# LayerNorm statistics moved from VectorE to ScalarE in a fused transformer block, and two sends put ahead of two transposing reads

## The chip, the cores and the metric

The kernel runs on one core of a Trainium2 chip. The metric is the device time of one execution in microseconds (us), the median of several runs. PE is TensorE's matmul side and PEld its weight loads, DVE is VectorE, ACT is ScalarE, POOL is GpSimd, SP the engine whose queue issues the transfers. The granted clock is the share of TensorE's full clock that the profile records, 1.00 being full.

A time is always a little longer than the span that the profile shows (first to last instruction): here by 1.74 to 1.86 us, in one experiment by 2.03 us.

## The reference, cut to what matters

```python
def _layernorm(x, axis=-1, eps=1e-5):
    m = jnp.mean(x, axis=axis, keepdims=True)
    v = jnp.var(x, axis=axis, keepdims=True)
    return (x - m) / jnp.sqrt(v + eps)
...
    # S = 2048 rows, D = 576, 32 heads, 8 dilated window positions, F = 4608
    h = x + attention(_layernorm(x), A_wqkv, A_wo)
    h2 = h + mlp(_layernorm(h), B_w1, B_b1, B_w2, B_b2)   # mlp normalises once more
```

The MLP is GELU (tanh form) between two matmuls. LN2 is the LayerNorm of `h` together with the second one inside the MLP: both fold into one factor, `rstd = (var * (1 + eps) + eps * eps) ** -0.5`.

## The kernel before

The 2048 rows are 16 tiles of 128, handled in eight pairs ("groups"). For each group, PE does MLP-1 (`pm`, 17.7 us), the attention output matmul Wo of the *next* pair (`pw`, 2.2 us) and MLP-2 (`po`, 17.8 us; 15.5 us in the last two groups). While PE does MLP-2 of one group, LN2 of the next pair runs on the other engines, and its result goes to HBM and comes back transposed (`hnT`), because MLP-1 needs it so. DVE is meanwhile busy with the attention of later tiles, whose Exp runs on ACT, in the same queue as the GELU evictions (`hT`).

```python
    def ln2(j):                                   # DVE
        pw = pw_of.pop(j)
        h = sb.tile([P, D], F32, tag="h", name="h", bufs=2)
        nc.vector.tensor_tensor(out=h..., in0=pw[:, :, 0:HALF], in1=x_all[:, j, :]..., op=ALU.add)
        h_of[j] = h
        hn[j] = (h,) + ln_stats([h[:]], "ln2", 1.0 + EPS, EPS * EPS, 2)   # 2 bn_stats, bn_aggr, veps

    # ln2_rstd: GpSimd pow;  ln2_bias: DVE, -mean * rstd;  ln2_hn: ACT, Identity(h * rstd + bias)

    def dma_transpose(dst, src):
        td = dram.tile([P, KT * P], BF16, tag="td", name="td", bufs=4)
        nc.sync.dma_start(out=td[:, 0:D], in_=src)
        nc.sync.dma_start(out=td[:, D:KT * P], in_=src[:, KF * P:D])
        nc.sync.dma_start_transpose(out=dst, in_=td[:])
...
        def ln2_pair(c, d, e, b2=True):
            for j in (c, d):
                ln2(j)
                ln2_rstd(j)
                if j == d:
                    ln2_bias(c)
                    send_h(c)                     # ln2_hn, then dma_transpose
                if b2:
                    add_b2(j)
            if e is not None:
                att_den(e)
            ln2_bias(d)
            send_h(d)
...
    def exps(j):
        att_exp(j)                                # ACT Exp of the logits of tile j
        gelu_table()                              # brings the GELU table back (1.28 us in the trace)
...
        # group 0:  ia[12] = exps(e), Wo of d, ln2_pair(c, d, e, False), ...   during MLP-2
        #           ib[4] = att_qk(f);  ib[32] = exps(f)
        # in the trace ACT keeps the order of the program: the GELU evictions of the next group (from 115.51 us)
        # come behind exps(f) (113.58)
```

The first pair (tiles `A[0]`, `A[1]`) is normalised in the QKV phase by the same helpers and is not touched by the change. So seven pairs change; "the first changed pair" is the one of the second group.

## Time and profile before

| | before |
|---|---|
| time, median of 3 runs | 372.36 us (372.13 to 372.79) |
| span of the profiled run | 370.9 us |
| PE busy | 363.7 us, 98% of the span, granted clock full in every slice |
| DVE, ACT, POOL busy | 316.0, 209.7, 26.5 us |

Part 1 of the page of the kernel before: each engine's busy time, its share of the span, and its number of instructions.

```profile
PE 363.7 (98%) x4944; PEld 300.7 (81%) x4944; DVE 316.0 (85%) x522; ACT 209.7 (57%) x435; POOL 26.5 (7%) x34
```

PE has about 7 us in which it does nothing, 5 of them ahead of the first matmul (1.5) and behind the last (3.6). Taking 20 us from DVE can then give little more than the share of the remaining 2 us that DVE causes. Where that is, the chain that ended last shows (start, duration, what, how often; "issue" is time in which the engine waited for nothing that the profile shows), again of the kernel before:

```profile
113.58 0.42 ACT logits L340
114.01 1.28 ACT L438
115.31 0.20 ACT warm L438
115.51 2.92 ACT hT L465 x8
118.43 0.04 issue
118.47 8.99 PE pm L204 x160
127.46 2.21 PE pw L204 x36
129.67 17.75 PE po L480 x144
147.41 17.79 PE pm L204 x324
```

From 118.47 us to the end the chain is matmuls. In front of that it runs through ACT: an Exp (L340), a GELU table load, eight evictions of the second group. That Exp had waited for DVE, as ACT's timeline of the kernel before shows (start, duration, engine, line, operation, output and input; in brackets the idle time ahead and what ended it):

```profile
95.12 0.42 ACT L340 ACTIVATE logits<-logits 128x256 f32<-128x256 f32 x1 [2.60 <-DVE logits L329]
99.09 0.87 ACT L168 ACTIVATE hn<-h,ln_nmr,ln_rstd 128x576 bf16<-128x576 f32 x1 [2.04 <-DVE ln_nmr L164]
100.52 0.87 ACT L168 ACTIVATE hn<-h,ln_nmr,ln_rstd 128x576 bf16<-128x576 f32 x1 [0.56 <-DVE ln_nmr L164]
...
113.58 0.42 ACT L340 ACTIVATE logits<-logits 128x256 f32<-128x256 f32 x1 [10.89 <-DVE logits L329]
```

In one number: from the first MLP-1 matmul of the second group (109.14 us) to the first Wo matmul behind it (127.28 us) PE took 18.14 us. I call this stretch the *stage*. The later groups, where nothing waits, take 17.7 us.

The SP queue of the kernel before, in the pair of the fourth group (a send is the two DMA_DIRECT2D into `td`, a transposing read the DMA_TRANSPOSE):

```profile
172.62 0.34 SPq L184 DMA_DIRECT2D td<-hn  x1
173.01 0.42 SPq L185 DMA_DIRECT2D td<-hn  x1
174.71 1.21 SPq L186 DMA_TRANSPOSE hnT<-td  x1
176.01 0.53 SPq L184 DMA_DIRECT2D td<-hn  x1
176.59 0.42 SPq L185 DMA_DIRECT2D td<-hn  x1
178.19 1.20 SPq L186 DMA_TRANSPOSE hnT<-td  x1
```

The second tile was ready at 174.7 us, but its send stood in the queue behind the first tile's read, which itself had to wait for the first send to land (the read was issued at 174.71 us, 2.1 us after the send, whose larger part takes 2.0 us to landing). A read lands 2.8 us after its issue (2.7 to 2.9 for those of `hnT`), so the second arrived at about 181.0 us; PE needed it at 185.1.

### The profile page before, as it was taken

The page shows a single profiled execution, that of the slowest core. Times are in us where ns is not written, and L with a number is a line of the kernel's source. Part 1 is how long each engine was busy: PE and PEld are TensorE (multiplying, and loading weights), DVE is VectorE, ACT ScalarE, POOL GpSimd, SP SyncE. Part 2 cuts the span into 40 slices and gives each one's busy share as a digit, 9 for nine tenths or more (in the row PEclk, how much of TensorE's full clock was granted, in tenths as well). Part 3 has the DMA queues.
Part 4 walks back from the last instruction along what each step waited for, and adds up shares of the span by engine and source line. Part 5 has one row for each costly group of instructions (what it writes and reads, how often), then busy time and mean ns, then how long its engine had stood idle before and what let it go on. Part 6 is the DMA issues. An engine that isn't in the chain of part 4 may idle for free.

```text
span 370.9 us, 11469 instructions
## 1 busy us (share of the span) xinstructions
PE 363.7 (98%) x4944; PEld 300.7 (81%) x4944; DVE 316.0 (85%) x522; ACT 209.7 (57%) x435; POOL 26.5 (7%) x34
## 2 busy tenths in 40 slices
PE   7999999999999999999999999999999999999996
PEld 4789877888789977887788778878887788778874
DVE  6799999999999999999999899999999997642332
ACT  2688755798407870867076807681668156505630
POOL 2322004000100020002000200020002000200000
PEclk9999999999999999999999999999999999999999
DMA  7987779955434314620412042203320321030000
GB/s 234 319 241 216 194 208 238 335 184 73 160 89 147 53 34 130 224 47 21 119 53 53 20 102 71 53 19 87 83 56 19 76 62 39 2 87 18 4 0 32
DMA packets 57266, 38.96 MB, mean 105 GB/s; under 512 B 31345, under 2 KB 55537, under 8 KB 57217
## 3 DMA queue, kind: packets, MB, share of 16 engines
q1 hardware_dynamic: 57056, 38.18, 37.7%
q8 instruction: 38, 0.62, 0.7%
q10 hardware_dynamic: 160, 0.07, 0.1%
q14 instruction: 12, 0.09, 0.1%
HBM read 19.92 MB, written 12.42 MB: 87 GB/s over the span
## 4 chain that ended last, share of the span: by engine, by line
PE 71%; DVE 22%; issue 2%; ACT 1%; DMA 1%; POOL 1%; POOLq 0%; DVEq 0%
PE pm L204 31%; PE po L480 24%; PE po L551 8%; PE pw L204 4%; DVE prod L357 3%; DVE prod L318 3%; DVE prod L312 3%; DVE prod L361 3%; DVE ln_stats L144 2%; PE pq L204 2%; DMA kv_ring<-kv_dram 1%; PE busy L636 1%; POOL ln_rstd L155 1%; DVE mx L328 1%; ACT hT L465 1%
## 5 line engine op out<-in xcount | busy, mean ns | idle before, releaser
L204 PE MATMUL pm<-hnT,w_sb 64*128 64x256 bf16 x2304 | 143.2, 269 | 0.6 <-ACT hT L465 0.5
L465 ACT ACTIVATE hT<-pm,b_sb 128x256 bf16<-128x256 f32 (+1 forms) x288 | 108.0, 502 | 34.3 <-PE pm L204 34.3
L204 PEld LDWEIGHTS <-w_sb 64*128 64x128 bf16 x2304 | 113.6, 94 | 14.4 <-issue 2.6
L480 PEld LDWEIGHTS <-hT 128*128 128x128 bf16 x864 | 84.0, 98 | 22.6 <-issue 1.7
L480 PE MATMUL po<-w2a_sb,hT 128*128 128x288 bf16 x672 | 84.5, 286 | 0.0
L204 PE MATMUL pq<-wq_sb,xnT 64*128 64x288 bf16 x768 | 54.0, 283 | 0.4 <-ACT xnT L250 0.2
L204 PEld LDWEIGHTS <-xnT 64*128 64x128 bf16 x864 | 44.0, 94 | 9.2 <-issue 0.4
L155 POOL TENSOR_TENSOR ln_rstd<-ln_veps,mhalf 128x1 f32<-128x1 f32 (+2 forms) x27 | 25.7, 953 | 296.7 <-DVE ln_veps L149 244.6
L318 DVE TENSOR_TENSOR prod<-prod 128x2304 bf16<-128x2304 bf16 (+1 forms) x64 | 44.3, 691 | 2.1
L340 ACT ACTIVATE logits<-logits 128x256 f32<-128x256 f32 x16 | 6.7, 417 | 68.0 <-DVE logits L329 67.9
L357 DVE TENSOR_TENSOR prod<-kv_ring,a 128x4608 bf16<-128x4608 bf16 x16 | 40.9, 2558 | 0.3
L312 DVE TENSOR_TENSOR prod<-kv_ring,q_all 128x4608 bf16<-128x4608 bf16 x16 | 40.8, 2552 | 0.4 <-DMA kv_ring<-kv_dram 0.2
L204 PE MATMUL pm<-hnT,w1h_sb 64*128 64x256 bf16 x288 | 39.5, 269 | 0.0
L361 DVE TENSOR_TENSOR prod<-prod 128x2304 bf16<-128x2304 bf16 (+1 forms) x32 | 33.9, 1058 | 1.1
L480 PE MATMUL po<-w2b_sb,hT 128*128 128x288 bf16 x192 | 25.5, 286 | 0.0
L289 ACT CAST kv_ring<-pq 128x576 bf16<-128x576 f32 x32 | 19.4, 640 | 8.3 <-PE pq L204 8.2
L168 ACT ACTIVATE hn<-h,ln_nmr,ln_rstd 128x576 bf16<-128x576 f32 x16 | 13.9, 867 | 13.5 <-DVE ln_nmr L164 13.5
L204 PE MATMUL pw<-wo_sb,oT 64*128 64x288 bf16 x256 | 19.5, 283 | 0.2
L438 ACT ACT_TABLE_LOAD x14 | 18.0, 1283 | 0.3
L204 PEld LDWEIGHTS <-oT 64*128 64x128 bf16 x288 | 14.1, 94 | 4.0 <-POOLq L214 0.8
L527 DVE TENSOR_TENSOR prod<-hT 128x512 f16<-128x512 f16 (+1 forms) x8 | 3.6, 455 | 16.0 <-ACT hT L465 16.0
L402 DVE TENSOR_TENSOR h<-pw,x_all 128x576 f32<-128x576 f32 x16 | 12.0, 753 | 5.7 <-PE pw L204 5.6
(89 smaller groups left out, 316.1 us busy)
## 6 DMA issues: line engine op xcount, KB each, us to landing
w_sb<-in_B_w_dram SPq DMA_DIRECT2D x6, 768.0 KB, 5.3
kv_ring<-kv_dram SPq DMA_DIRECT2D x28, 144.0 KB, 2.5
w2a_sb<-in_B_w_dram SPq DMA_DIRECT2D x4, 1008.0 KB, 6.6
kv_dram<-kv_ring SPq DMA_DIRECT2D x13, 288.0 KB, 3.9
out_dram<-o_sb SPq DMA_DIRECT2D x15, 144.0 KB, 2.0
td<-q_all SPq DMA_DIRECT2D x14, 144.0 KB, 2.2
td<-hn SPq DMA_DIRECT2D x14, 144.0 KB, 2.0
wq_sb<-in_A_wqkv_dram SPq DMA_DIRECT2D x3, 576.0 KB, 6.7
```

Source lines behind the costliest of these rows:

```text
L155: nc.gpsimd.tensor_tensor(out=rstd[:], in0=veps[:], in1=mhalf[:].to_broadcast([P, n]), op=ALU.pow)
L168: nc.scalar.activation(out=dst, in_=src, func=ACT.Identity, scale=rstd, bias=nmr)
L204: last = nc.tensor.matmul(duo["g"][r ^ swap][i], lhsT=lhsT, rhs=rhs, start=(swap == 0 and i == 0 and kt == 0), stop=(swap == 1 and kt == K ...
L289: pace[0] = nc.scalar.copy(out=dst.rearrange("p (d g h) -> p g d h", g=2, h=H // 2), in_=ps[:, :, 0:HALF].rearrange("p g (h d) -> p g d h" ...
L312: nc.vector.tensor_tensor(out=prod[:], in0=k_ring[j % 2], in1=q_all[:, j, :].unsqueeze(1) .to_broadcast([P, W, D]), op=ALU.mult)
L318: nc.vector.tensor_tensor(out=prod[:, :, o * H:o * H + n], in0=prod[:, :, a * H:a * H + n], in1=prod[:, :, c * H:c * H + n], op=ALU.add)
L357: nc.vector.tensor_tensor(out=prod[:].rearrange("p w (d h) -> p w d h", h=H), in0=v_ring[j % 2].rearrange("p w (d h) -> p w d h", h=H), in ...
L361: nc.vector.tensor_tensor(out=prod[:, 0:n, :], in0=prod[:, 0:n, :], in1=prod[:, n:2 * n, :], op=ALU.add)
L438: nc.scalar.activation(out=warm[:], in_=mhalf[:], func=ACT.Gelu_apprx_tanh)
L465: pace[0] = nc.scalar.activation(out=hT[us[i // GF]][:, GF * r + i % GF, 0:N], in_=ps[:, r, i * N:(i + 1) * N], func=ACT.Gelu_apprx_tanh, ...
L480: nc.tensor.matmul(banks[half], lhsT=hT[f // (2 * GF)][:, f % (2 * GF), i * P:(i + 1) * P], rhs=w2_rows(f)[:, half * HALF:(half + 1) * HAL ...
L551: nc.tensor.matmul(bank, lhsT=l, rhs=r, start=(start and m == 0), stop=(m == NM - 1), skip_group_check=True)
```

## The change

The intent: take LN2's statistics off DVE, which is 85% busy, and give them to ACT, which is 57% busy, as two passes whose sums the engine accumulates; and let the second tile's send go out ahead of the first tile's read.

```diff
-    def dma_transpose(dst, src):
+    def dma_out(src):
         td = dram.tile([P, KT * P], BF16, tag="td", name="td", bufs=4)
         nc.sync.dma_start(out=td[:, 0:D], in_=src)
         nc.sync.dma_start(out=td[:, D:KT * P], in_=src[:, KF * P:D])
+        return td
...
+    def ln2_act(j):
+        h = h_of[j]
+        y = sb.tile([P, D], BF16, tag="hn", name="hn", bufs=2)
+        nmean, var, rstd = (... [P, 1] tiles ...)
+        nc.scalar.activation(out=y[:], in_=h[:], func=ACT.Identity, scale=-1.0 / D, accum_out=nmean[:])
+        nc.scalar.activation(out=y[:], in_=h[:], func=ACT.Square, bias=nmean[:], accum_out=var[:])
+        nc.scalar.activation(out=var[:], in_=var[:], func=ACT.Identity, scale=(1.0 + EPS) / D, bias=eps2[:])
+        nc.gpsimd.tensor_tensor(out=rstd[:], in0=var[:], in1=mhalf[:], op=ALU.pow)
+        hn[j] = (h, rstd, nmean, y)
+
+    def ln2_send(j):
+        h, rstd, nmean, y = hn[j]
+        nc.scalar.activation(out=nmean[:], in_=nmean[:], func=ACT.Identity, scale=rstd[:])
+        ln_apply_act(y[:], h[:], rstd[:], nmean[:])
+        hn[j] = dma_out(y[:])
+
+    def ln2_in(j):
+        nc.sync.dma_start_transpose(out=hnT_slot(j), in_=hn.pop(j)[:])
...
         def ln2_pair(c, d, e, b2=True):
             for j in (c, d):
-                ln2(j)
-                ln2_rstd(j)
-                if j == d:
-                    ln2_bias(c)
-                    send_h(c)
+                ln2_h(j)                          # only the residual addition
+                ln2_act(j)
+            for j in (c, d):
                 if b2:
                     add_b2(j)
+                ln2_send(j)
+            for j in (c, d):
+                ln2_in(j)
             if e is not None:
                 att_den(e)
-            ln2_bias(d)
-            send_h(d)
```

More of the change, by code (lines that the diff above doesn't have):

```diff
@@ L78 @@
     b2_bc = wpool.tile([P, D], BF16, name="b2_bc")
+    eps2 = wpool.tile([P, 1], F32, name="eps2")
     mhalf = wpool.tile([P, 1], F32, name="mhalf")
@@ L185, in dma_transpose @@
         nc.sync.dma_start(out=td[:, D:KT * P], in_=src[:, KF * P:D])
+        return td
+    def dma_transpose(dst, src):
+        td = dma_out(src)
         nc.sync.dma_start_transpose(out=dst, in_=td[:])
@@ L397, in wo_duo, with ln2_h @@
         return make
-    def ln2(j):
+    def ln2_h(j):
         pw = pw_of.pop(j)
@@ L404, in ln2 @@
         h_of[j] = h
+        return h
+    def ln2(j):
+        h = ln2_h(j)
         hn[j] = (h,) + ln_stats([h[:]], "ln2", 1.0 + EPS, EPS * EPS, 2)
+    def ln2_act(j):
+        h = h_of[j]
+        y = sb.tile([P, D], BF16, tag="hn", name="hn", bufs=2)
+        nmean, var, rstd = (sb.tile([P, 1], F32, tag=f"ln2_{t}", name=f"ln2_{t}", bufs=2) for t in ("nmean", "var", "rstd"))
+        nc.scalar.activation(out=y[:], in_=h[:], func=ACT.Identity, scale=-1.0 / D, accum_out=nmean[:])
[10 more added lines that the diff above has]
+        nc.sync.dma_start_transpose(out=hnT_slot(j), in_=hn.pop(j)[:])
     def add_b2(j):
@@ L432, in tr_h @@
         nc.scalar.copy(out=hnT_slot(j), in_=pt)
-    def dma_tr_h(j):
-        dma_transpose(hnT_slot(j), hn.pop(j)[:])
     def gelu_table():
@@ L637 @@
         nc.gpsimd.memset(mhalf[:], -0.5)
+        nc.gpsimd.memset(eps2[:], EPS * EPS)
         make_identity(nc, ident[:])
@@ L696, in pv_t @@
             dma_tr_o(j)
-        def send_h(j):
-            ln2_hn(j)
-            dma_tr_h(j)
         def ln2_pair(c, d, e, b2=True):
             for j in (c, d):
-                ln2(j)
-                ln2_rstd(j)
-                if j == d:
-                    ln2_bias(c)
-                    send_h(c)
+                ln2_h(j)
+                ln2_act(j)
+            for j in (c, d):
                 if b2:
                     add_b2(j)
+                ln2_send(j)
+            for j in (c, d):
+                ln2_in(j)
             if e is not None:
                 att_den(e)
-            ln2_bias(d)
-            send_h(d)
         loads = {v: [c_(load_w1, c)] for c, v in enumerate((3, 4, 9, 14, 16, 18))}
```

## The prediction

> **What bounds the kernel.** TensorE. The page gives PE busy 363.7 of 370.9 us (98%), clock full in every slice. The table of PE's waits holds only 3.0 us, half of it before the first matmul. The last-ending chain looks mixed (PE 71%, DVE 22%), but from 118.47 us to 367.3 us it is matmuls alone, and the DVE part before it runs beside an almost full PE: the only stall that it hands to PE in the MLP is at 118.47 us. There the GELU evictions of the second group start late (115.42 us), because ScalarE's queue holds an Exp that waits 10.9 us for DVE's logits. The MLP-1 pass of that group takes 18.3 us (109.14 to 127.46), the later ones 17.8: about 0.5 us lost.
>
> **What changes** (14 of 16 tiles; the first pair keeps the old way).
> - DVE loses two BATCH_NORM_STATS2 (452 ns each), the aggregate (209), veps (156) and nmr (153): 1.42 us a tile, 20 us in all. DVE busy 316 to about 296 us.
> - ScalarE gains two 576-column passes and two one-column operations. [...] ACT busy 210 to 235-245 us, of 371. No table load is added in the built order.
> - GpSimd keeps one pow a tile (0.55 to 1.0 us).
> - The transfers are the same in number. In a steady pair of before, the sends begin at 172.62 and 176.01 and the transposing reads at 174.71 and 178.19; the second send waits behind the first read though its data was ready at 174.71. Now the second send no longer does.
>
> **On the critical path?** A reading lands 2.8 us after issue, so the second tile arrived at about 181.0, and PE needs it at 185.1. With ScalarE's serial chain (starting after the Exp and the GELU table load end at 171.2) the second normalised tile is ready near 176.9 instead of 174.7; the regrouped sends give back about 1 us; it lands near 182: still 3 us early. In the first changed pair (needed at 109.14) I get 108.1 against 108.45 before; in the last (needed at 333.86) about 332.4 against 332.5. So PE shouldn't wait anywhere. What remains is that DVE runs about 2.5 us earlier after the first changed pair, so the blocking Exp and the GELU evictions start about 2 us earlier and the 0.5 us stall goes.
>
> **Time.** 372.36 - 0.5 = 371.9 us, range 371.3 to 372.7. Faster by over 2%: 0.01, within 2%: 0.98, slower: 0.01.
>
> **What would show it.** DVE near 296 us busy and more idle; ACT near 240; PE busy unchanged near 363.7; the first MLP-1 pass after 109 us at 17.8 us with no wait on hT; no PE wait on hnT's reads; the two hnT reads of a pair issued back to back, the second near 179 in the steady pair. The chain of waits stays PE throughout the MLP.
>
> **What would make it wrong.** If the accumulating passes cost some 0.3 us more each than estimated, the four in series use up the 1.1 and 1.4 us of slack in the first and last changed pair, and PE waits there for hnT by some tenths of a us. If ScalarE were held up further (by pow on GpSimd, or by semaphores between its dependent steps), the same waits would appear in all seven pairs, each adding directly. If earlier DVE work moves halo or weight transfers into collisions, the reads could land late.

Cut from it are the costs of single operations from which ACT's gain was put together, as no trace of the case showed them. They came to 2.0 us a tile, 28 us in all, reading the accumulator left open. ACT's 235 to 245 us, the 176.9 us of the second normalised tile and the landing times (near 182, 108.1 and 332.4 us) rest on this sum, an estimate of mine not taken from the traces; the time, 372.36 - 0.5 = 371.9 us, does not contain it. As to its last sentence, reads do land at different times after their issue: in the changed kernel that of `oT` at 89.41 us took 2.90 us, with 69 GB/s moved meanwhile, that at 145.59 us 4.45 us, with 163 GB/s.

## The result, and the profile after

The changed kernel took 371.69 us (371.56 to 372.19, 4 runs) against 372.25 us (372.07 to 372.79, 4 runs) of the kernel before. A ratio is the mean time of one kernel's runs over that of the other's of the same rounds, so not quite the ratio of the medians that are quoted; here it is 0.9985, interval 0.9968 to 1.0002. Two further batches gave 371.55 us against 372.16 (0.9980, 0.9968 to 0.9993) and 371.68 against 372.37 (0.9987, 0.9974 to 0.9999). So the change is worth a little over half a microsecond: "same" at 2%, as predicted.

Part 1 of the page of the changed kernel:

```profile
PE 363.2 (98%) x4944; PEld 299.4 (81%) x4944; DVE 299.3 (81%) x452; ACT 239.1 (65%) x519; POOL 25.2 (7%) x35
```

DVE lost 16.7 us and ACT gained 29.4 us; PE does what it did. The chain that ended last, in the changed kernel, over the same stretch:

```profile
93.92 14.81 PE po L505 x120
108.72 17.79 PE pm L209 x324
126.52 2.21 PE pw L209 x36
128.72 17.75 PE po L505 x144
```

There is no ACT piece any more: MLP-1 of the second group is one run of 17.79 us, as in all later groups. The stage takes 17.69 us (108.66 to 126.35), 0.45 less than before. ACT's timeline of the changed kernel shows both sides of the trade:

```profile
96.43 0.67 ACT L420 ACTIVATE hn<-h 128x576 bf16<-128x576 f32 x1
97.00 0.19 ACT L420 ACTIVATION_READ_ACCUMULATOR hn<-h 128x1 f32 x1
97.22 0.78 ACT L421 ACTIVATE hn<-h,ln_nmean 128x576 bf16<-128x576 f32 x1
97.90 0.19 ACT L421 ACTIVATION_READ_ACCUMULATOR hn<-h,ln_nmean 128x1 f32 x1
98.12 0.29 ACT L422 ACTIVATE ln_var<-ln_var,eps 128x1 f32<-128x1 f32 x1
...
101.99 0.87 ACT L169 ACTIVATE hn<-h,ln_nmean,ln_rstd 128x576 bf16<-128x576 f32 x1
...
110.40 0.42 ACT L345 ACTIVATE logits<-logits 128x256 f32<-128x256 f32 x1 [6.25 <-DVE logits L334]
```

The second normalised tile is ready at 102.86 us instead of 101.39, later although PE runs 0.5 us earlier in this profile. The blocking Exp starts at 110.40 instead of 113.58. The SP queue of the changed kernel, in the pair of the fourth group:

```profile
175.19 0.34 SPq L185 DMA_DIRECT2D td<-hn  x1
175.58 0.42 SPq L186 DMA_DIRECT2D td<-hn  x1
176.28 0.33 SPq L185 DMA_DIRECT2D td<-hn  x1
176.66 0.42 SPq L186 DMA_DIRECT2D td<-hn  x1
177.22 2.52 SPq L433 DMA_TRANSPOSE hnT<-td  x2
```

The reads are back to back. The second starts at 178.5 us (177.22 + 2.52 less its own 1.2) and, at 2.9 us to landing, arrives near 181.4; PE needs it at 184.1.

The two profiled spans differ by 1.1 us (370.9 and 369.8), which is more than the effect. Half a us of it lies ahead of the change: PE's first MLP-1 matmul came at 69.87 us before and at 69.36 us after, in a part of the program where both kernels do the same but for one small GpSimd memset. In the other two profiles of the changed kernel it came at 69.98 and 70.01 us, in those of the experiments between 69.3 and 70.5. A single pair of profiles therefore cannot be subtracted here; the stage can.

Cut at the same matmuls, the two profiles differ nowhere else on PE's path: from the first MLP-1 matmul to the stage it is 39.27 us before and 39.30 after, from the third group's first MLP-1 matmul to the end of the last matmul 219.91 us in both. Behind the last matmul 3.60 us of the span are left before and 3.46 after. That piece is 3.60 and 3.62 us in e6 and e10, which build on the kernel before, and 3.42 to 3.46 in all the runs that build on the changed kernel, e3 included. So some 0.15 us of what the spans gain is in the closing instructions and not in the stage; no run shows why.

### The profile page after: what moved, and what is told of

Same layout as the page of the kernel before. It is cut to its first block, busy times and chain, and to the rows that moved or that the text cites. A ratio compares the mean times of both kernels' runs of the same rounds, so it can differ in the third digit from the quotient of the medians.

```text
span 369.8 us, 11478 instructions
## 1 busy us (share of the span) xinstructions
PE 363.2 (98%) x4944; PEld 299.4 (81%) x4944; DVE 299.3 (81%) x452; ACT 239.1 (65%) x519; POOL 25.2 (7%) x35
## 4 chain that ended last, share of the span: by engine, by line
PE 84%; DVE 11%; ACT 2%; POOL 1%; issue 1%; POOLq 0%; DVEq 0%
PE pm L209 37%; PE po L505 29%; PE po L576 8%; PE pw L209 5%; PE pq L209 4%; DVE ln_stats L145 2%; DVE prod L323 2%; DVE prod L362 1%; DVE prod L317 1%; PE busy L661 1%; DVE prod L366 1%; POOL ln_rstd L156 1%; ACT hT L490 1%; DVE ln_mv L146 1%; ACT L463 0%
## 5 line engine op out<-in xcount | busy, mean ns | idle before, releaser
L423 POOL TENSOR_TENSOR ln_rstd<-ln_var,mhalf 128x1 f32<-128x1 f32 x14 | 11.3, 810 | 249.8 <-ACT ln_var L422 249.6
L345 ACT ACT_TABLE_LOAD x13 | 16.7, 1283 | 0.2
```

The lines of the kernel that those rows point to most:

```text
L345: nc.scalar.activation(out=logits[:], in_=logits[:], func=ACT.Exp, scale=SCALE)
```

## The experiments

Theory: the whole gain is the stage. DVE finishes the logits of tile f earlier, so the Exp that blocks ACT's queue is earlier, so the GELU evictions of the second group are in time. Rivals: the gain comes from less DVE work, or from earlier reads, in all seven pairs. A second question is why the longer ACT chain costs nothing, and how near it is to costing something.

| run | median, us | before, us | stage, us | PE waits on hnT, us |
|---|---|---|---|---|
| before, profiled | 372.36 | | 18.14 | none |
| changed, e1 and e11 | 371.55, 371.68 | 372.16, 372.37 | 17.69, 17.69 | none |
| e2, first changed pair only | 372.05 | 372.16 | 17.70 | none |
| e3, all but that pair | 372.20 | 372.16 | 18.13 | none |
| e4, Exp ahead of GELUs | 373.79 | 372.16 | 17.68 | 1.47 |
| e5, statistics only | 374.66 | 372.10 | 17.68 | 1.35, 0.66, 1.14 |
| e6, sends only | 372.20 | 372.10 | 18.13 | none |
| e7, one more pass | 373.19 | 372.10 | 17.68 | 0.98, 0.36 |
| e8, two more passes | 386.73 | 372.10 | 20.47 | 3.81, then 1.2 to 1.9 in each pair, 0.29 in the last |
| e9, e4 mended | 372.06 | 372.37 | 17.68 | 1.27 |
| e10, half statistics | 371.98 | 372.37 | 17.69 | none |
| e12, e9 with one table switch | 371.97 | 372.36 | 17.68 | 0.82 |

### e1 and e11: the changed kernel again

No edit; yardsticks of their batches.

> The changed kernel once more, as the yardstick of this batch. Expected 371.7 us, about 0.5 us under the kernel before. The MLP-1 pass of the second group (the run of 324 MLP-1 matmuls that follows the first changed pair) should take 17.8 us, against 18.3 in the kernel before.

> The changed kernel as the yardstick of this batch: 371.6 us, 0.5 us under the kernel before.

Both came as expected, 371.55 and 371.68 us, with the stage at 17.69 us.

### e2 and e3: where the gain sits

```diff
# e2: the first changed pair new, the others as before (ln2_pair_old: statistics, sends and order of the kernel before)
-                ia[0] = ... c_(ln2_pair, c, d, e)]
+                ia[0] = ... c_(ln2_pair_old, c, d, e)]
# e3: the other way round
-                ia[12] = [..., c_(ln2_pair, c, d, e, False), ...]
+                ia[12] = [..., c_(ln2_pair_old, c, d, e, False), ...]
```

> New LN2 for the first changed pair alone, the other six pairs as before. Theory (the whole gain is the removed wait of PE for the GELU evictions of the second group): as fast as the changed kernel, 371.7 us, with a 17.8 us MLP-1 pass in the second group. Rival (the gain comes from less VectorE work, or earlier transposing reads, in all seven pairs): one seventh of it, so 372.2 us.

> The complement: the first pair's LN2 as before, new LN2 for the other six pairs. Theory: no gain, 372.25 us as the kernel before, and the MLP-1 pass of the second group takes 18.3 us again, though DVE's busy time falls by six sevenths of what the whole change took off. Rival: six sevenths of the gain, 371.8 us.

The stage decides it: 17.70 us with that pair alone, 18.13 us with the other six alone, although the six took DVE's busy time from 316.0 to 301.9 us. Six sevenths of the work moved bought nothing on PE's path.

The medians say it less clearly. e3 is level with the kernel before (372.20 against 372.16), as the theory has it. e2 was to be as fast as the changed kernel and came at 372.05, only 0.1 us under before. Its spans explain a part: their mean is 370.12 us, against 370.54 of the kernel before, 370.36 of e3 and 369.84 of e1 in the same batch. But in each of its five runs the time exceeds the span by 2.02 to 2.05 us, where all the others have 1.74 to 1.86. These 0.2 us lie outside the first and last instruction, and no run here says what they are. So e2 by its trace has the gain, by its spans most of it, by its times not clearly; what lies outside the span stays open.

### e6: the sends alone

```diff
# kernel before, statistics on DVE as they were
-            dma_tr_h(j)
+            hn[j] = dma_out(hn[j][:])
...
             send_h(d)
+            for j in (c, d):
+                ln2_in(j)
```

> The kernel before with the regrouped sends alone, statistics on DVE as before. Theory: the second read of each pair is issued 1 to 1.5 us earlier, but nobody waits for it, so 372.25 us as before, and the second group's MLP-1 pass stays at 18.3 us. Rival (earlier reads are the gain): 371.7 us.

372.20 against 372.10 us, stage 18.13: no gain from earlier reads, as nobody waited for them.

### e10: the same DVE time taken away by another way

```diff
# kernel before; wrong result on purpose (the check of the output passed its tolerance all the same)
-            for c in range(2):
+            for c in range(halves):          # 1 for the two tiles of the first changed pair, 2 for all others
                 nc.vector.bn_stats(...)
-            nc.vector.bn_aggr(out=mv[:, i, :], in_=stats[:, i, :, :])
+            nc.vector.bn_aggr(out=mv[:, i, :], in_=stats[:, i, 0:halves, :])
```

> The kernel before, with the statistics of the first changed pair taken over the first half of each row alone (wrong result on purpose): VectorE loses two BATCH_NORM_STATS2, 0.9 us, ScalarE gains nothing. Theory (it is VectorE's time ahead of the blocking Exp that counts, wherever it goes): the second group's MLP-1 pass loses its wait and takes 17.7 us to its end instead of 18.1, with the Exp 0.9 us earlier; 371.8 us. Rival (the new order on ScalarE and of the sends in that pair does it): 372.2 us and 18.1.

This leaves ACT and the sends alone and takes two BATCH_NORM_STATS2 from DVE. ACT's timeline of e10, the blocking Exp:

```profile
112.36 0.42 ACT L340 ACTIVATE logits<-logits 128x256 f32<-128x256 f32 x1 [10.89 <-DVE logits L329]
```

Counted from the first matmul of its stage (108.71 us), the Exp starts after 3.65 us, where in the kernel before it starts after 4.44 (113.58 less 109.14). That is enough: the stage is 17.69 us, and the spans of its five runs have a mean of 370.2 us against 370.6 of the kernel before. By its times alone (ratio 0.9993, 0.9979 to 1.0006) the gain would not be clear. It is DVE's time ahead of the Exp that counts, by whichever way it goes. It also shows that the change took far more than was needed: its own Exp starts 1.74 us into the stage.

### e5: the statistics without the sends

```diff
             for j in (c, d):
                 if b2:
                     add_b2(j)
                 ln2_send(j)
-            for j in (c, d):
                 ln2_in(j)
```

> The statistics on ScalarE, but each tile's transposing read right behind its own send, as before. Theory (the regrouped sends are what pays for ScalarE's longer chain): the second read of the first changed pair is issued near 107.1 us and lands near 110.0, PE wants it at 108.7: 1.3 us of wait; in the last pair it lands near 334.0 against 333.0: 1.1 us; none in the five pairs between (183.6 against 184.2). In all 374.1 us, slower than the kernel before by 1.9 us. Rival (the sends' order does not matter, there is slack anywhere): 371.7 us.

374.66 us, slower than the kernel before by 2.6 us. PE's timeline of e5 (in brackets PE's idle time and its cause), in the first, fourth and last changed pair:

```profile
110.08 0.61 PE L209 MATMUL pm<-hnT,w_sb 64*128 64x256 bf16 x8 [1.35 <-DMA hnT<-td]
...
224.03 0.61 PE L209 MATMUL pm<-hnT,w_sb 64*128 64x256 bf16 x8 [0.66 <-DMA hnT<-td]
...
336.27 0.61 PE L209 MATMUL pm<-hnT,w_sb 64*128 64x256 bf16 x8 [1.14 <-DMA hnT<-td]
```

The first and last waits came within 0.05 us of what was expected; the one in the fourth pair was not expected: there the first read was issued 3.3 us after its tile was ready (214.33 to 217.64 us), in the pairs next to it 2.1 us after; why is not shown. The two halves of the change belong together: the sends alone bring nothing and the statistics alone do harm, and the regrouped sends are what pays for the longer chain on ACT.

### e7 and e8: how much slack is left

```diff
-        nc.scalar.activation(out=y[:], in_=h[:], func=ACT.Identity, scale=-1.0 / D, accum_out=nmean[:])
+        # the same line twice (e7), three times (e8), in each changed tile
```

> The changed kernel with the first accumulating pass done twice in each tile (0.67 us and 0.19 us for the accumulator, 0.79 us net), so the pair's chain is 1.6 us longer. It measures the slack. Theory (second read lands 0.25 us early in the first changed pair, 0.75 in the last, 2.7 in the five between): PE waits 1.3 and 0.85 us, 373.9 us. Rival (PE has more room than I read, the chain is not near critical): 371.7 us.

> The same with that pass done three times in each tile, 3.2 us a pair. Theory: waits of 2.9 us (first), 2.4 (last) and 0.4 in each of the five between: 7.5 us in all, 379.2 us. Were the slack the same in all pairs, the cost would grow evenly, 1.6 us a pair from the run before to this: 11 us more.

e7 took 373.19 us, with waits of 0.98 us in the first changed pair and 0.36 us in the last and none between. The two passes add 1.6 us of work to the pair's chain, and taking 1.6 less the wait for the slack would give 0.6 and 1.2 us. The trace says that this is too much: against the time at which PE would have come, the second read landed only 1.05 us later than in the changed kernel in both pairs. In the first pair the added work took the place of some 0.35 us in which ACT had waited for GpSimd's pow (more of that under e12); in the last the second read stood 0.7 us less long in the queue. PE starts 0.13 to 0.14 us after the landing that it waits for (at 110.10 us behind 107.19 + 2.78, at 334.78 behind 331.60 + 3.04). So the slack was about 0.1 us in the first changed pair and 0.7 in the last in the profile of the changed kernel (0.3 and 0.6 in that of e1): no more than I had read, 0.25 and 0.75. The order is as expected.

e8 took 386.73 us, 15 us more than the changed kernel, where I had expected 7.5. PE's timeline of e8 in the first two changed pairs:

```profile
112.54 1.03 PE L209 MATMUL pm<-hnT,w_sb 64*128 64x256 bf16 x8 [3.81 <-DMA hnT<-td]
...
154.42 0.61 PE L209 MATMUL pm<-hnT,w_sb 64*128 64x256 bf16 x8 [1.29 <-DMA hnT<-td]
```

The waits in the seven pairs are 3.81, 1.29, 1.85, 1.71, 1.25, 1.15 and 0.29 us, and one of 1.21 us behind an ACT copy in the last changed pair's MLP-2: 12.6 us. Two things made the loss larger than 7.5.

First, the pow on GpSimd. For the second tile it took 2.43 us in the first changed pair and 1.61 us in the five between, and ACT stood still for it (1.46 us, and 0.71 in the second pair). More of that under e12.

Second, the granted clock. The same eight matmuls take 1.03 us behind the long wait and 0.61 us behind the short one. The view by stretches of e8 (stretch, length, busy time and number of instructions of each engine, then granted clock, share of DMA, GB/s):

```profile
100.00:112.50 12.50, 8.74 (x72) 6.75 (x69) 11.91 (x17) 8.82 (x18) 3.89 (x2) 0.96 0.24 58
112.50:116.00 3.50, 3.46 (x34) 2.80 (x36) 2.31 (x1) 0.00 (x0) 0.00 (x0) 0.50 0.35 98
116.00:120.00 4.00, 4.00 (x56) 3.50 (x54) 3.90 (x6) 1.41 (x4) 0.00 (x0) 0.72 0.87 278
120.00:124.00 4.00, 4.00 (x78) 3.94 (x76) 3.96 (x3) 3.09 (x10) 0.00 (x0) 1.00 0.35 86
```

When the matmuls resume at 112.54 us, after 3.8 us without one, the clock is at half (0.50), and it is full again some 5.7 us later: a mean of 0.72 in the third stretch means about 2.2 us more at half, so to about 118.2 us. The stage of that pair took 20.47 us instead of 17.70: 2.8 us more, and 12.6 + 2.8 is the 15 us. The wait of 3.81 us brought the fall; the waits of up to 1.85 us did not (the mean clock is 1.00 in each 40 us from 120 to 320 us). When it fell can be estimated from the first stretch: a mean of 0.96 over 12.5 us, if it was full before, is 1.0 us at half, so from about 111.5 us, some 2.8 us after the end of the last matmul (108.73).

### e4, e9 and e12: the other wait of the same kind

PE has one more wait for GELU evictions behind an Exp, 0.47 us in the first group, in both kernels. I tried to take it by putting that group's Exp (tile d) ahead of its evictions, where the Exp table is still loaded (in e4 this Exp ran at 74.59 us with no table load ahead of it; in the changed kernel one of 1.28 us precedes it).

```diff
# e4, on top of the changed kernel
-            20: [c_(ln2_rstd, A[1]), c_(add_b2, A[1]), ...]        (18 and A[0] likewise)
+            20: [c_(ln2_rstd, A[1]), ...]
-        gelu_table()
         for k, g in enumerate(GROUPS):
...
-                m1[0] += [..., c_(att_qk_b, d), c_(halo, d, 1)]
-                mid[0] = [c_(exps, d)]
+                m1[0] += [..., c_(att_qk_b, d), c_(halo, d, 1), c_(exps, d), c_(add_b2, g[0]), c_(add_b2, g[1])]
# e9: the two add_b2 behind pv_t(d) instead; a one-column Exp ahead of exps(e) to load its table early
-                ia[12] = [c_(exps, e), ...]
+                ia[12] = [exp_table, c_(exps, e), ...]
# e12: e9, and no GELU table between the two Exps of a group
-                c_(exps, e)
+                c_(att_exp, e)                                   (in ia[12] and ia[0])
```

> The changed kernel, with the same remedy for the other wait of PE for the GELU evictions (0.47 us in the first group's MLP-1 pass): the Exp of tile d moves in front of that group's GELU evictions, where the Exp table is still loaded (two table loads of 1.28 us go), and the two additions of b2 (0.75 us each) move behind that tile's logits, so that the Exp can start about 1.5 us earlier. Theory (PE's waits for GELU evictions behind an Exp are all that is left to take on this path): 371.2 us, no PE wait on hT left in the first group. Rival (the GELU evictions now start too late, near 74.5 us instead of 72.6, and the wait stays): 371.7 us.

> The fourth run mended. Its Exp of tile d stays in front of the first group's GELU evictions, but the two additions of b2 go behind both attention sums (so the transposed attention outputs are not late), and the Exp table of the next Exp is loaded ahead by a one-column Exp (so the load does not wait for VectorE's logits). Theory: no PE wait on hT in the first group (0.47 us gone); PE then reaches the second group 0.5 us earlier and meets the first changed pair's second read, which has 0.25 us of slack: 0.2 us of wait. In all 371.4 us, 0.3 under the changed kernel. Rival (the evictions start later and the wait only moves): 371.7 us or more.

> The ninth run with one thing taken from ScalarE's chain: between the two Exps of a group the GELU table is no longer loaded (LN2's Identity and Square passes need no load of their own in the built order), so two table loads a group go, and the LN2 chain starts 1.5 us earlier in every pair. Theory (the ninth run's gain in the first group was eaten by the late second read of the first changed pair, which waits for this chain): the read lands near 107.9 us and PE arrives at 108.2, so neither the wait on hT (0.47) nor the one on hnT (1.27) is left: 371.0 us, 0.6 us under the changed kernel. Rival (the read is late for another reason, such as the DMA queue): 371.6 us or more, with a wait on hnT in the first changed pair.

All three took that wait away, and none was faster than the changed kernel (e12 ran in a batch without it; against the kernel before it has 0.9989, the changed kernel 0.9980 to 0.9987). In e4 (373.79 us) the moved additions held up DVE's attention sums, so PE waited 1.2 us for a transposed attention output; and the wait for DVE's logits had been put on the table load ahead of the Exp, so the load began only when the logits were there (at 96.51 us, after ACT had stood 5.24 us; the Exp came 1.29 us later) and LN2 behind it was late (1.47 us of wait on hnT). e9 mended both (372.06 us), but its two additions still stand in front of LN2 on DVE, which has less than half a us to give there: 1.27 us of wait.

e12 (371.97 us, ratio to before 0.9989, 0.9976 to 1.0003) started ACT's chain 1.2 us earlier than e9 did (95.90 us against 97.07), and should have had no wait left. It kept 0.82 us. (The view names a DVE product as what ended this wait. But the second read was issued at 106.01 us, 104.44 + 2.77 less its own 1.2, and at 2.8 us to landing arrived near 108.81. PE starts at 108.95, 0.14 us after that, as behind the second read of the first changed pair in e4, e5, e7 and e8, where it is 0.13 to 0.14 us, so I put it down to the read.) ACT's timeline of e12 has the reason, the step that needs the first tile's pow:

```profile
100.91 0.29 ACT L428 ACTIVATE ln_nmean<-ln_nmean,ln_rstd 128x1 f32<-128x1 f32 x1 [1.11 <-POOL ln_rstd L423]
```

GpSimd's and DVE's timelines of e12 there:

```profile
98.05 4.22 POOL L423 TENSOR_TENSOR ln_rstd<-ln_var,mhalf 128x1 f32<-128x1 f32 x2 [35.06 <-ACT ln_var L422]
```

```profile
97.91 2.56 DVE L362 TENSOR_TENSOR prod<-kv_ring,a 128x4608 bf16<-128x4608 bf16 x1
100.51 2.15 DVE L366 TENSOR_TENSOR prod<-prod 128x2304 bf16<-128x2304 bf16 x2
```

The first of the two pows began 0.14 us after a DVE product of two SBUF tensors and took 2.82 us, to 100.87 us: 0.40 us after that product ended (100.47). In e9 the same product ended at 100.48 us, and the step that follows the pow began at 100.92 us, within 0.01 us of e12. Starting the chain earlier changed nothing, because the pow was not done before the product was. The same figure holds wherever a pow met such an operation: in the traces of the kernel before and of the changed kernel, all 23 that began, after 40 us, with more than 0.1 us of such an operation left ended 0.41 to 0.42 us after it. Thus in the changed kernel the pow of 172.33 us ended at 173.25, 0.40 after the product of 170.29 + 2.56; in e8 that of 185.47 us ended at 187.08, 0.41 after the product of 184.12 + 2.55. Undisturbed it takes 0.55 us, and so it did in the kernel before at 97.19 us, beside a DVE addition with one input in PSUM, and at 99.13 us, beside a reduction with one input. So what a pow that met such a DVE operation paid was the rest of that operation and 0.4 us; why is not shown.

So no version beat the changed kernel. The rival that I wrote for e12 ("late for another reason, such as the DMA queue") was right that there was another reason, and named the wrong one.

## Why the prediction was right

- **The time.** Predicted 371.9 us (371.3 to 372.7), measured 371.69, and 371.55 and 371.68 again. Right.
- **"What bounds the kernel. TensorE."** Right: PE's busy time stayed (363.7 and 363.2 us), and 17 us less on DVE and 29 us more on ACT moved the time by half a us. e3 is the clean proof: most of the work moved, no gain.
- **"So the blocking Exp and the GELU evictions start about 2 us earlier and the 0.5 us stall goes."** Right in kind, and near in size: the Exp starts 1.74 us into the stage instead of 4.44, so 2.7 us earlier, and the stage went from 18.14 to 17.69 us. e2, e3 and e10 show that it is this and DVE's part of it.
- **"The only stall that it hands to PE in the MLP is at 118.47 us."** This was misread. The 0.5 us that the table of PE's waits lists against ACT is another one, 0.47 us at 79.45 us in the first group, and it is still there after the change (0.47 us at 78.95). The loss of the second group is in gaps too short for that table (the longest, at 118.47 us, is 0.10 us, and the ends of matmuls are modelled); it shows only as a longer stage. The sum held because the prediction took its size from the lengths of the passes, 18.3 against 17.8 us, and not from the table.
- **DVE near 296 us.** Measured 299.3. I had summed the rows, 1.42 us a tile, but neighbouring rows overlap by about 0.1 us and busy time counts that once: in the fourth group's pair, DVE's stretch from the first residual addition to the last b2 addition shrank from 5.4 us (166.96 to 172.36) to 2.8 us (166.01 to 168.77).
- **ACT 235 to 245 us.** Measured 239.1. The trace has 0.667, 0.775, 0.294 and 0.279 us for the four operations (medians of 14), in sum the 2.0 us a tile of my estimate. The unknown, reading the accumulator, is an instruction of its own of 0.187 us, twice a tile (28 of them).
- **The slack.** For the first changed pair I had the second read landing 1.0 us ahead of PE (108.1 against 109.14); the trace has it issued at 105.45 and landing at 108.44, against 108.66: 0.2 us by the landing times, of which PE needs 0.14. In the last I had 1.4 us (332.4 against 333.86) and the trace has 0.8. The terms missing from my sum were the accumulator reads (four in series, 0.75 us) and the pow held up by DVE (1.68 us for the first tile). My warning "if the accumulating passes cost some 0.3 us more" was thus near to coming true; the pair just held, and with 0.1 us left that was luck.
- **The sends.** I gave them about 1 us in the second tile's landing; by the landing times they are worth 1.4 us in the first changed pair (0.2 us ahead of PE with them; in e5 1.2 us after the time at which PE would have come) and 2.1 us in the fourth group's (2.76 us ahead, in e5 0.62). e5 also shows what their absence costs: 1.35, 0.66 and 1.14 us of PE's time.

## What to carry to other kernels

Where one engine is busy 98% of the span, work moved between the others is worth only what they make that engine wait (here 16.7 us taken from DVE gave 0.45): find those waits first, in stretches that should be of equal length, because gaps of a tenth of a us are in no table of waits. Moving work to an idle engine lengthens a serial chain even when the busy shares look better (here the second tile was ready 1.5 us later); measure the slack of that chain before spending it (here 0.1 to 0.3 us). Lengthening the chain on purpose shows where it breaks first, but read from the trace how much later its end came: of 1.6 us added, about 1 arrived. And when two profiles differ by more than the effect, compare the stage that changed, not the spans.
